# First head pair of an attention and two-MoE kernel: a new order of the start, head by head

## The chip, the cores and the metric

One core of a Trainium2 chip runs the whole program in one launch. The metric is device time in microseconds (us). The kernel before takes 651.89 us as the median of three runs (651.56 to 652.99). Its engines are TensorE (PE), VectorE (DVE), ScalarE (ACT), GpSimd (POOL) and SyncE (SP), which issues most transfers. PEld rows are TensorE's weight loads.

## The reference, cut to what matters

Three stages follow each other: cluster attention, a dense MLP, a routed MoE. The change touches the attention alone, and there its first pair of heads.

```python
q, k, v: (2, 8, 768, 64)   centroids: (8, 16, 64)
q_assign = argmax(q_n @ c_n.T); k_assign = argmax(k_n @ c_n.T)      # 16 clusters
mask = q_assign[:, :, :, None] == k_assign[:, :, None, :]
scores = where(mask, (q @ k.T) / 8, -1e9)
attn = exp(scores - max); attn /= sum + 1e-9
x = (attn @ v)  ->  (1536, 512)
h = x @ w_in; g = max(0.01 * h, h); x2 = g @ w_out                  # dense MLP
out = x2 + gate * (relu(x2 @ w1[e]) @ w2[e])   where x2 @ w_skip > 0, e = argmax(x2 @ w_gate)
```

## The kernel before, in words

**Tiling.** The 16 heads are worked off as 8 pairs p of two heads h. A pair takes 12 steps: a step s is 128 query rows of one head against all 768 keys. In pair 0 the steps alternate between the heads (h = 0, 1, 0, 1, ...). A step issues scores on PE (`sps`, four matmuls: two over the U tile with K = 80, two over the V tile with K = 128), a row maximum on DVE (`st`), an exponential on ACT (`pr`), and three steps later six transposes on PE (`tps`) whose copies ACT writes to `pt`. After six steps probabilities times v follow (`avps`). The `sps` tile has two buffers, so the scores of step s wait for the exponential of step s - 2.

**High and low parts.** q and k are fp32. Each is split into a high part in fp32r (a copy) and a low part (a subtraction). The tiles of pair p hold them by partitions: UA is head 0's high part (partitions 0 to 63), UB head 1's, VA and VB hold what the second pair of score matmuls multiplies. Rows 64 to 79 of UA and UB are the cluster masks: one-hot rows of the keys (0 or 1) and of the queries (0 or -2^60). A mask mismatch so lowers a score by 2^60.

**Preparation of a pair.** Load q and k (`nat`, for pair 0 `first` and a copy to `nat`); transpose on PE (`rawps`); copy on ACT (`raw`); split; exchange halves between the tiles by transfers on SP; multiply by the normalised centroids (`cblk`, result `asps`); copy on ACT (`sc`); transpose (`scps`); argmax in five DVE operations (maximum, equal, times `cw`, maximum, equal, result `oh`); masks. For pairs 1 to 7 the preparation is spread over the steps of the pair before by the tables PREP and PREP1. For pair 0 it stands ahead of the loop, lines 481 to 531, and PE's first scores come behind all of it: the order in the source is the order on each engine, since nothing reorders instructions.

**Ahead of the loop, in order.** SP issues `first` for q, the centroids (`cnat`), `first` for k, then pair 1's `natq` and `natk`. DVE normalises the centroids (`cst`, `cexp`). The high parts of q are made on POOL (line 199), those of k on ACT (line 197), all low parts on DVE (line 497), nine transfers of 192 KB exchange halves. `prep_cblk` (line 162) transposes `cexp` and copies it to `cblk`. One argmax serves both heads (lines 249 to 270). `mask_first` (line 273) makes the masks of head 0, then of head 1: 12 small transposes each (`mps`), a copy on ACT for the keys, one or two operations on DVE for the queries. Pair 1's q and k are transposed and copied there too.

## Time and profile before

| | before |
|---|---|
| median of 3 runs | 651.89 us |
| profiled execution, its own time | 651.22 us |
| its span, first to last instruction | 649.3 us |
| PE busy | 631.6 us, 97% of the span |
| DVE, ACT, POOL busy | 441.4, 420.8, 165.9 us |

The profiled execution's own time is 1.9 us longer than its span, and 0.7 us under the median of the runs. A time in a row is counted from the span's start. In the page's row of 40 slices PE has a 5 in the first one (16 us) and a 9 in all but the last after it: the start is the only stretch of some length in which PE is not busy. A busy PE is not PE at its peak, since matmuls are pipelined.

### The profile page before, as it was taken

The numbers are of one execution on the slowest core, as the hardware profiler recorded it, in microseconds if no ns is written. First come the engines' busy times: TensorE is split into PE (matmuls) and PEld (weight loads), VectorE is DVE, ScalarE is ACT, GpSimd is POOL, SyncE is SP. The second block draws the span as 40 slices with busy tenths as digits, with TensorE's granted clock in tenths as the row PEclk, the third lists the DMA queues.
The fourth block names the chain that finished last, engine by engine and source line by source line (L and its number), as shares of the span: only waits on it lengthen the run. The fifth ranks groups of instructions, "written<-read, shape, count | busy, mean of one in ns | idle before, by whom it ended". The sixth has DMA issues, their size and how long they took to land.

```text
span 649.3 us, 10059 instructions
## 1 busy us (share of the span) xinstructions
PE 631.6 (97%) x3599; PEld 489.9 (75%) x3599; DVE 441.4 (68%) x767; ACT 420.8 (65%) x829; POOL 165.9 (26%) x215
## 2 busy tenths in 40 slices
PE   5999999999999999999999999999999999999994
PEld 3777776776777676888888888888788878688874
DVE  6756868687777754988755355645566448999971
ACT  5788898898888885654544444444564346688860
POOL 4233647373655424300000000000000025004311
PEclk9999999999999999999999999999999999999998
DMA  8766566677656427223004000006234438999930
GB/s 194 183 188 160 144 167 186 154 202 187 189 174 172 156 71 276 97 98 100 1 1 194 1 1 0 2 12 248 108 131 150 140 131 304 365 349 373 360 136 28
DMA packets 63636, 99.53 MB, mean 153 GB/s; under 512 B 27697, under 2 KB 31763, under 8 KB 63200
## 3 DMA queue, kind: packets, MB, share of 16 engines
q1 hardware_dynamic: 60304, 90.62, 44.7%
q0 software_dynamic: 3280, 8.24, 3.7%
q8 instruction: 29, 0.48, 0.3%
q14 instruction: 23, 0.19, 0.1%
HBM read 72.73 MB, written 12.70 MB: 132 GB/s over the span
## 4 chain that ended last, share of the span: by engine, by line
PE 92%; ACT 2%; POOL 2%; DVE 1%; DMA 1%; issue 1%; SPq 0%; POOLq 0%
PE ups L669 20%; PE acc L775 19%; PE sps L371 10%; PE avps L443 10%; PE tps L428 8%; PE hps L1273 7%; PE yps L1304 7%; PE rawps L179 1%; PE hT L1285 1%; PE acc L1165 1%; PE x2T L859 1%; ACT pr L389 1%; PE asps L232 1%; DMA recip_scratch<-rrow 1%; PE scps L244 1%; PE xT L1034 1%
## 5 line engine op out<-in xcount | busy, mean ns | idle before, releaser
L374 DVE TENSOR_REDUCE st<-sps 128x1 f32<-128x768 f32 x96 | 91.6, 955 | 51.8 <-PE sps L371 50.9
L435 ACT ACTIVATE pt<-tps 128x384 f32<-128x384 f32 x192 | 85.5, 511 | 17.8 <-PE tps L428 16.6
L389 ACT ACTIVATE pr<-sps,st 128x768 f32<-128x768 f32 x96 | 88.2, 919 | 11.5 <-DVE st L374 11.2
L428 PE MATMUL tps<-ident,pr 128*128 128x128 f32 x576 | 79.0, 273 | 0.5 <-ACT pt L435 0.5
L669 PE MATMUL ups<-xh,whii 128*128 128x512 f32 x192 | 74.8, 390 | 0.0
L669 PE MATMUL ups<-xh,wloi 128*128 128x512 f32 x192 | 74.7, 389 | 0.0
L669 PE MATMUL ups<-xl,whii 128*128 128x512 f32 x192 | 74.7, 389 | 0.0
L775 PE MATMUL acc<-whio,gh 128*128 128x512 f32 x183 | 73.0, 399 | 0.0
L428 PEld LDWEIGHTS tps<-ident,pr 128*128 128x128 f32 x576 | 67.8, 140 | 5.8 <-ACT pt L435 1.6
L443 PE MATMUL avps<-pt,vnat 128*64 128x384 f32 x384 | 72.1, 498 | 0.0
L775 PE MATMUL acc<-whio,gl 128*128 128x512 f32 x183 | 71.4, 390 | 0.0
L775 PE MATMUL acc<-wloo,gh 128*128 128x512 f32 x183 | 71.3, 390 | 0.0
L760 ACT ACTIVATE gh<-g 128x512 fp32r<-128x512 f32 x48 | 30.4, 633 | 43.5 <-DVE g L759 43.5
L758 ACT ACTIVATE lk<-ups 128x512 f32<-128x512 f32 x48 | 28.4, 592 | 36.8 <-PE ups L669 30.3
L759 DVE TENSOR_TENSOR g<-ups,lk 128x512 f32<-128x512 f32 x48 | 33.0, 688 | 28.3 <-ACT lk L758 28.2
L762 DVE TENSOR_TENSOR gl<-g,gh 128x512 fp32r<-128x512 f32 x48 | 33.2, 691 | 25.2 <-ACT gh L760 25.2
L1013 POOL DMA_INDIRECT xe<-x_scratch,eix x1 | 1.2, 1165 | 190.0 <-DVE eix L1012 190.0
L646 DVE TENSOR_TENSOR wloi<-rawb,whii 128x512 fp32r<-128x512 f32 x36 | 24.8, 689 | 27.5 <-ACT whii L645 27.4
L443 PEld LDWEIGHTS avps<-pt,vnat 128*64 128x64 f32 x384 | 23.4, 136 | 25.5 <-issue 25.0
L669 PEld LDWEIGHTS ups<-xh,whii 128*128 128x128 f32 x192 | 36.0, 188 | 8.1 <-issue 0.6
L669 PEld LDWEIGHTS ups<-xl,whii 128*128 128x128 f32 x192 | 36.0, 188 | 7.5
L669 PEld LDWEIGHTS ups<-xh,wloi 128*128 128x128 f32 x192 | 36.0, 188 | 7.5
(303 smaller groups left out, 1358.3 us busy)
## 6 DMA issues: line engine op xcount, KB each, us to landing
rawb<-in_moe_w_dram SPq DMA_DIRECT2D x25, 1024.0 KB
rawa<-in_moe_w_dram SPq DMA_DIRECT2D x10, 1024.0 KB
stg<-in_moe_w_in_dram SPq DMA_DIRECT2D x16, 512.0 KB
stg<-in_moe_w_out_dram SPq DMA_DIRECT2D x16, 512.0 KB
UB<-UA SPq DMA_DIRECT2D x16, 192.0 KB
...
```

The costliest lines, as they stand in the source:

```text
L371: nc.tensor.matmul(ps[:, kh, 0:HS], lhsT=t[0:n, 0, qs], rhs=t[0:n, 1, kh * HS:(kh + 1) * HS], start=first, stop=not first)
L374: nc.vector.tensor_reduce(out=st[:, 0:1], in_=ps[:, :, 0:HS], axis=AX.XY, op=ALU.max, negate=True)
L389: nc.scalar.activation(out=pr, in_=ps[:, :, 0:HS], func=AF.Exp, bias=st[:, 0:1], accum_out=sm_t[g][:, 3 * h + j:3 * h + j + 1])
L428: nc.tensor.transpose(ps[:, t, :], pr[:, kh, t * P:(t + 1) * P], ident)
L435: nc.scalar.activation(out=pt[:, 3 * kh:3 * kh + 3, j, :], in_=t_t[s][kh], func=AF.Copy)
L443: nc.tensor.matmul(av_t[g][64 * h:64 * h + 64, :], lhsT=vnat[p][:, h, kt, :], rhs=pt_t[p, half, h][:, kt].rearrange("p j c -> p (j c)"), s ...
L669: nc.tensor.matmul(ps, lhsT=w[:, cc, :], rhs=x[:, blk, cc, :], start=(n == 0), stop=(n == 3 * KD - 1))
L759: nc.vector.tensor_tensor(out=g, in0=ps, in1=t, op=ALU.max)
L762: nc.vector.tensor_tensor(out=gl, in0=g, in1=_f(gh), op=ALU.subtract)
L775: nc.tensor.matmul(ps, lhsT=a[:, ts_], rhs=w, start=(fc == 0 and n == 0), stop=(fc == NFC - 1 and n == 2))
L1273: nc.tensor.matmul(ps, lhsT=x[:, c, :], rhs=w, start=(n == 0), stop=(n == len(mm) - 1))
L1304: nc.tensor.matmul(ps[:, cs], lhsT=x[:, f, :], rhs=w[:, cs], start=(h == 0 and f == 0 and n == 0), stop=(h == 1 and f == 3 and n == 2))
```

## The change

It changes the work ahead of the loop and steps 0 to 11.

- The centroids are loaded from ACT's queue instead of SP's, so k's load is the second on SP.
- The copies of head 0's q to `nat` move from DVE to POOL.
- Head by head: the first six steps are head 0's three, then head 1's three (`where`). Splits are made by head, over 64 partitions and 768 elements, instead of by half, over 128 partitions and 384 elements. Low parts of head 0 are on DVE, those of head 1 on POOL. Six transfers replace nine.
- The argmax is made by head with operations half as large: head 0's five ahead of step 0, head 1's first two ahead of step 0 and three behind the maxima of steps 0 and 1. Masks likewise; head 1's are made after step 2's scores. The copy of a key mask is shared between ACT and DVE.
- Pair 1's third and fourth group of transposes move from ahead of the loop into steps 1 and 2, as do the load of v (step 0) and of pair 2's q and k (step 2); pair 1's assignment moves from step 1 to step 3.
- Matmuls of the identity with itself (`wps`) are put on PE: 6 at the very start, 1, 2, 6 and 4 ahead of step 0, 5, 2 and 6 in steps 1 and 2. Their results are not used.
- The new tiles `first_lo` and `first_hi` take buffers of `pr`, as `lo_k` did.

DVE in the stretch of the splits and of the argmax, before. `VA` and `lo_k` are low parts, `cblk` the normalised centroids that PE waits for.

```order
L159 TENSOR_SCALAR cexp<-cnat,cst,par 128x64 x2
L497 TENSOR_TENSOR VA<-raw,UA 128x384
L165 COPY cblk<-cps 128x128
L497 TENSOR_TENSOR VA<-raw,UA 128x384
L497 TENSOR_TENSOR lo_k<-raw,UA 128x384 x2
L251 TENSOR_REDUCE mx<-scps 128x24
```

The same stretch of DVE after, to the end of head 0's masks.

```order
L159 TENSOR_SCALAR cexp<-cnat,cst,par 128x64 x2
L221 TENSOR_TENSOR VA<-raw,UA 64x768
L165 COPY cblk<-cps 128x128
L221 TENSOR_TENSOR first_lo<-raw,UA 64x768
L306 TENSOR_REDUCE mx_207<-scps 128x12
L311 TENSOR_TENSOR eq<-scps,mx_207 128x12x16
L315 TENSOR_TENSOR eq<-eq,cw 128x12x16
L317 TENSOR_REDUCE mx_207<-eq 128x12
L319 TENSOR_TENSOR oh<-eq,mx_207 128x12x16
L306 TENSOR_REDUCE mx_234<-scps 128x12
L336 CAST UA<-mps 16x384
L340 TENSOR_SCALAR UA<-mps 16x128
```

Two subtractions of 768 elements stand where four of 384 stood, and one of them is still ahead of `cblk`; the argmax has the same five operations at half the size.

DVE in steps 0 to 2 after, behind the masks that step 0 needs. `st` is a step's maximum, `UB` holds head 1's masks. Before, the two operations for UB's queries and UA's were ahead of step 0, and four maxima stood in a row.

```order
L311 TENSOR_TENSOR eq<-scps,mx_234 128x12x16
L431 TENSOR_REDUCE st<-sps 128x1 x2
L340 TENSOR_SCALAR UA<-mps 16x384
L315 TENSOR_TENSOR eq<-eq,cw 128x12x16
L317 TENSOR_REDUCE mx_234<-eq 128x12
L319 TENSOR_TENSOR oh<-eq,mx_234 128x12x16
L431 TENSOR_REDUCE st<-sps 128x1
L336 CAST UB<-mps 16x384
L340 TENSOR_SCALAR UB<-mps 16x768
L431 TENSOR_REDUCE st<-sps 128x1 x3
```

The three last operations of head 1's argmax and its masks now stand between the maxima of steps 1, 2 and 3.

ACT from step 0 on, after: `pr` is an exponential, `raw` a copy for pair 1, `UB` the first half of head 1's key mask, `pt` a copy of transposes, `sc` pair 1's assignment.

```order
L446 ACTIVATE pr,sm<-sps,st 128x768 x2
L196 ACTIVATE raw<-rawps 128x384
L335 ACTIVATE UB<-mps 16x384
L446 ACTIVATE pr,sm<-sps,st 128x768
L196 ACTIVATE raw<-rawps 128x384
L492 ACTIVATE pt_364<-tps 128x3x128 x2
L446 ACTIVATE pr,sm<-sps,st 128x768
L260 ACTIVATE sc<-asps 128x384
```

Before, `raw` and the masks came ahead of the first `pr`, and `sc` behind the second. The diff, without the parts that the list above tells in full:

```diff
@@ -190,13 +195,30 @@
         sc = SCALE if qk == 0 else 1.0
         nc.scalar.activation(out=raw_t[p][:, i, :], in_=ps, func=AF.Copy, scale=sc)
 
-    def first_hi(i):
-        qk, half = divmod(i, 2)
-        hi, src = uv_t[0][0][:, qk, half * HS:(half + 1) * HS], raw_t[0][:, i, :]
-        if qk:
-            nc.scalar.activation(out=hi, in_=src, func=AF.Copy)
-        else:
-            nc.gpsimd.tensor_scalar(out=hi, in0=src, scalar1=1.0, scalar2=1.0, op0=ALU.mult, op1=ALU.mult)
+    first_t = {}
+
+    def first_raw(qk, h):
+        return raw_t[0][64 * h:64 * h + 64, 2 * qk:2 * qk + 2, :].rearrange("p a b -> p (a b)")
+
+    def first_hi(qk, h, again=False):
+        U, W, X, Y = uv_t[0]
+        if qk == 0:
+            dst = (Y if h else U)[64 * h:64 * h + 64, 0, :]
+            nc.gpsimd.tensor_scalar(out=dst, in0=first_raw(0, h), scalar1=1.0, scalar2=1.0, op0=ALU.mult, op1=ALU.mult)
+        else:
+            dst = first_t["hi"][64:128] if h else (X if again else U)[0:64, 1, :]
+            nc.scalar.activation(out=dst, in_=first_raw(1, h), func=AF.Copy)
+
+    def first_lo(qk, h):
+        U, W, X, Y = uv_t[0]
+        if qk == 0:
+            hi = (Y if h else U)[64 * h:64 * h + 64, 0, :]
+            dst = first_t["lo"][64:128] if h else X[0:64, 0, :]
+        else:
+            hi = first_t["hi"][64:128] if h else U[0:64, 1, :]
+            dst = Y[64:128, 1, :] if h else first_t["lo"][0:64]
+        eng = nc.gpsimd if h else nc.vector
+        eng.tensor_tensor(out=dst, in0=first_raw(qk, h), in1=_f(hi), op=ALU.subtract)
 
     def raw_split(p, i):
         raw = raw_t[p]
@@ -270,21 +292,53 @@
                                 op=ALU.is_equal)
         oh_t[p] = oh
 
-    def mask_first(h):
-        U = uv_t[0][h]
+    def by_head(ap, h):
+        return ap.rearrange("p j (a h) c -> p j a h c", h=2)[:, :, :, h, :]
+
+    am0 = {}
+
+    def argmax_first(h, i):
+        V = nc.vector
+        sc = by_head(ps_prep["am"], h)
+        sh = [P, 3, 4, NC_]
+        if i == 0:
+            am0["m", h] = att_a.tile([P, 3, 4], F32, tag="mx0", name="mx0", bufs=2)
+            V.tensor_reduce(out=am0["m", h], in_=sc, axis=AX.X, op=ALU.max)
+        elif i == 1:
+            if "e" not in am0:
+                am0["e"] = att_a.tile([P, 3, 8, NC_], F32, tag="eq", name="eq")
+                oh_t[0] = att_a.tile([P, 3, 8, NC_], BF16, tag="oh", name="oh")
+            V.tensor_tensor(out=by_head(am0["e"], h), in0=sc, in1=am0["m", h].unsqueeze(3).to_broadcast(sh),
+                            op=ALU.is_equal)
+        elif i == 2:
+            eq = by_head(am0["e"], h)
+            V.tensor_tensor(out=eq, in0=eq, in1=cw[:, 0:4].unsqueeze(1).to_broadcast(sh), op=ALU.mult)
+        elif i == 3:
+            V.tensor_reduce(out=am0["m", h], in_=by_head(am0["e"], h), axis=AX.X, op=ALU.max)
+        else:
+            V.tensor_tensor(out=by_head(oh_t[0], h), in0=by_head(am0["e"], h),
+                            in1=am0["m", h].unsqueeze(3).to_broadcast(sh), op=ALU.is_equal)
+
+    mf_t = {}
+
+    def mask_first_pe(h):
         for qk in (1, 0):
-            ps = (ps_m if h else ps_t)([P, S], "mps", BF16) if qk or not h else ps_a([P, S], "mps", BF16)
+            ps = ps_t([P, S], "mps", BF16)
             for i in range(2):
                 for j in range(3):
                     o = (3 * i + j) * P
                     nc.tensor.transpose(ps[64:64 + NC_, o:o + P], oh_t[0][:, j, 4 * qk + 2 * i + h, :], identb)
-            ps = ps[64:64 + NC_, :]
-            if qk:
-                nc.scalar.activation(out=U[64:64 + NC_, 1, :], in_=ps, func=AF.Copy)
-            else:
-                for cs in (slice(0, HS), slice(HS, S)) if h == 0 else (slice(0, S),):
-                    nc.vector.tensor_scalar(out=U[64:64 + NC_, 0, cs], in0=ps[:, cs], scalar1=BIG, scalar2=-BIG,
-                                            op0=ALU.mult, op1=ALU.add)
+            mf_t[h, qk] = ps[64:64 + NC_, :]
+
+    def mask_first_k(h):
+        U, ps = uv_t[0][h], mf_t[h, 1]
+        nc.scalar.activation(out=U[64:64 + NC_, 1, 0:HS], in_=ps[:, 0:HS], func=AF.Copy)
+        nc.vector.tensor_copy(U[64:64 + NC_, 1, HS:S], ps[:, HS:S])
+
+    def mask_first_q(h, a, z):
+        U, ps = uv_t[0][h], mf_t[h, 0]
+        nc.vector.tensor_scalar(out=U[64:64 + NC_, 0, a:z], in0=ps[:, a:z], scalar1=BIG, scalar2=-BIG,
+                                op0=ALU.mult, op1=ALU.add)
 
     def mask_pe(p):
         ps = (ps_t if p == 2 else ps_m)([P, 3, P], "ohps", BF16)
@@ -325,8 +379,9 @@
     PREP = plan(1)
     PREP0 = [(3, "a0", assign_act, None), (3, "pb", argmax_pe, None), (4, "d", argmax_0, None), (4, "d", argmax_1, None),
              (5, "d", argmax_2, None), (6, "d", argmax_3, None)]
-    PREP1 = [(1, "pb", assign_pe, None), (2, "a0", assign_act, None), (2, "pb", argmax_pe, None), (3, "pb", argmax_0, None), (4, "pb", argmax_1, None), (5, "d", argmax_2, None), (6, "pb", argmax_3, None), (7, "pb", mask_pe, None), (8, "d", mask_dve, None),
-             (8, "d", mask_dma, None)]
+    PREP1 = [(3, "pb", assign_pe, None), (4, "a0", assign_act, None), (4, "pb", argmax_pe, None),
+             (5, "d", argmax_0, None), (5, "d", argmax_1, None), (6, "d", argmax_2, None), (7, "d", argmax_3, None),
+             (8, "pb", mask_pe, None), (8, "pb", mask_dve, None), (8, "pb", mask_dma, None)]
     PREPS = {0: PREP0, 1: PREP1, 2: plan(5)}
 
     def prep(p, r, slot):
@@ -359,6 +414,8 @@
         p, r = divmod(s, 12)
         half, r = divmod(r, 6)
         j, h = divmod(r, 2)
+        if s < 6:
+            h, j = divmod(s, 3)
         return p, half, j, h
 
     def st_scores(s):
...
@@ -485,50 +547,47 @@
     for i in range(4):
         raw_pe(0, i)
         raw_act(0, i)
-    for i in range(4):
-        first_hi(i)
-    UA, UB, VA, VB = uv_t[0]
-
-    lo_k = att.tile([P, 2, HS], F32R, tag="pr", name="lo_k", bufs=4)
-
-    def first_lo(qk, halves=(0, 1)):
-        for half in halves:
-            cs = slice(half * HS, (half + 1) * HS)
-            nc.vector.tensor_tensor(out=lo_k[:, half, :] if qk else VA[:, 0, cs], in0=raw_t[0][:, 2 * qk + half, :],
-                                    in1=_f(UA[:, qk, cs]), op=ALU.subtract)
-
-    Uq, Wq, Xq, Yq = (_f(t[:, 0, :]) for t in (UA, UB, VA, VB))
-    Uk, Wk, Xk, Yk = (_f(t[:, 1, :]) for t in (UA, UB, VA, VB))
-    nc.sync.dma_start(Wq[0:64], Uq[64:128])
-    nc.sync.dma_start(Yq[64:128], Uq[64:128])
-    nc.sync.dma_start(Wk[0:64], Uk[64:128])
-    nc.sync.dma_start(Yk[0:64], Uk[64:128])
-    first_lo(0, (0,))
+    U, W, X, Y = uv_t[0]
+    for nm in ("lo", "hi"):
+        t = att.tile([P, 2, HS], F32R, tag="pr", name="first_" + nm, bufs=4)
+        first_t[nm] = t.rearrange("p a b -> p (a b)")
+    first_hi(0, 0)
+    nc.sync.dma_start(_f(X[64:128, 0, :]), _f(U[0:64, 0, :]))
+    first_hi(0, 1)
+    nc.sync.dma_start(_f(W[0:64, 0, :]), _f(Y[64:128, 0, :]))
+    first_lo(0, 0)
     prep_cblk()
-    first_lo(0, (1,))
-    nc.sync.dma_start(Yq[0:64], Xq[64:128])
-    nc.gpsimd.dma_start(Xk[0:64], Uk[0:64])
+    warm_pe(1, wps)
+    first_hi(1, 0)
+    first_hi(1, 1)
     assign_pe(0)
-    first_lo(1)
-    lo_kf = _f(lo_k.rearrange("p a b -> p (a b)"))
-    nc.sync.dma_start(Xk[64:128], lo_kf[0:64])
-    nc.sync.dma_start(Yk[64:128], lo_kf[64:128])
-    nc.sync.dma_start(Xq[64:128], Uq[0:64])
+    warm_pe(2, wps)
+    first_lo(1, 0)
+    nc.sync.dma_start(_f(X[64:128, 1, :]), _f(first_t["lo"][0:64]))
     prep(0, 3, "a0")
+    first_hi(1, 0, True)
+    nc.sync.dma_start(_f(W[0:64, 1, :]), _f(first_t["hi"][64:128]))
+    nc.sync.dma_start(_f(Y[0:64, 1, :]), _f(first_t["hi"][64:128]))
+    first_lo(0, 1)
+    nc.sync.dma_start(_f(Y[0:64, 0, :]), _f(first_t["lo"][64:128]))
     nc.scalar.activation(out=warm, in_=warm, func=AF.Exp)
     prep(0, 3, "pb")
-    for r in range(4, 7):
-        for slot in ("d", "pb"):
-            prep(0, r, slot)
-    load_v(0)
-    for i in range(4):
-        raw_pe(1, i)
-        raw_act(1, i)
-    load_qk(2)
-    mask_first(0)
-    mask_first(1)
-    for i in range(4):
-        split_first(1, i)
+    for i in range(5):
+        argmax_first(0, i)
+    raw_pe(1, 0)
+    raw_pe(1, 1)
+    wps = ps_a([P, P], "wps")
+    warm_pe(6, wps)
+    argmax_first(1, 0)
+    first_lo(1, 1)
+    mask_first_pe(0)
+    mask_first_k(0)
+    mask_first_q(0, 0, P)
+    mask_first_q(0, P, HS)
+    raw_act(1, 0)
+    raw_act(1, 1)
+    argmax_first(1, 1)
+    warm_pe(4, wps)
 
     chunks = {}
     ring_b = [None]
@@ -690,6 +749,29 @@
         p, r = divmod(s, 12)
         if s < NSTEP:
             st_scores(s)
+        if s == 0:
+            load_v(0)
+        elif s == 1:
+            raw_pe(1, 2)
+            warm_pe(5, wps)
+            mask_first_q(0, HS, S)
+            for i in range(2, 5):
+                argmax_first(1, i)
+        elif s == 2:
+            raw_act(1, 2)
+            raw_pe(1, 3)
+            warm_pe(2, wps)
+            mask_first_pe(1)
+            warm_pe(6, wps)
+            mask_first_k(1)
+            mask_first_q(1, 0, S)
+            load_qk(2)
+            for i in range(2):
+                split_first(1, i)
+        elif s == 3:
+            raw_act(1, 3)
+            for i in range(2, 4):
+                split_first(1, i)
         conv_step(s, 0)
         preps(p, r, "a0")
         preps(p, r, "pa")

```

## Rows read from the trace of the kernel before

**Rows 1.** Waits of PE from 24 to 645 us: total, times, longest us
```profile
PE tps L428 <- ACT pt L435: 0.5, 2, 0.3
PE rcps L406 <- ACT raw L191: 0.3, 1, 0.3
```

**Rows 2.** Windows: length, busy us (instructions) by engine, granted clock, DMA share, GB/s
```profile
12.00:16.00 4.00, 2.86 (x17) 2.46 (x16) 3.39 (x5) 2.39 (x6) 2.63 (x4) 1.00 1.03 236
24.00:28.00 4.00, 3.99 (x29) 3.44 (x27) 3.30 (x5) 4.00 (x11) 0.59 (x1) 1.00 0.56 139
```

**Rows 3.** Timeline of PE: start us, us, engine, line, operation, count, [idle before]
```profile
8.85 1.51 PE L232 MATMUL asps<-raw,cblk 128*32 128x384 f32 x8 [0.58 <-DVE cblk L165]
10.98 0.90 PE L244 MATMUL scps<-ident,sc 128*128 128x128 f32 x3 [0.63 <-ACT sc L238]
12.96 1.49 PE L179 MATMUL rawps<-ident,natk 128*128 128x128 f32 x6
15.58 2.73 PE L280 MATMUL mps<-identb,oh 128*16 128x128 bf16 x24 [1.14 <-DVE oh L269]
18.24 1.01 PE L371 MATMUL sps<-UA 80*128 80x384 f32 x2
...
23.41 0.60 PE L371 MATMUL sps<-UB 80*128 80x384 f32 x2
...
24.19 0.81 PE L428 MATMUL tps<-ident,pr 128*128 128x128 f32 x6
24.89 0.62 PE L371 MATMUL sps<-UA 80*128 80x384 f32 x2
...
33.10 0.62 PE L371 MATMUL sps<-UB 80*128 80x384 f32 x2
```

**Rows 4.** Timeline of SP: issues of the first loads
```profile
1.31 0.46 SPq L107 DMA_DIRECT2D cnat<-in_centroids_dram  x1
1.80 0.43 SPq L103 DMA_DIRECT2D first<-in_k_dram  x1
```

**Rows 5.** Timeline of ACT, start to step 1
```profile
6.04 0.61 ACT L475 ACTIVATE nat<-first 128x192 f32<-128x192 f32 x2 [1.15 <-DMA first<-in_k_dram]
...
6.56 2.03 ACT L191 ACTIVATE raw<-rawps 128x384 f32<-128x384 f32 x4
...
10.44 0.49 ACT L238 ACTIVATE sc<-asps 128x384 f32<-128x384 f32 x1 [1.03 <-PE asps L232]
...
20.80 0.90 ACT L389 ACTIVATE pr<-sps,st 128x768 f32<-128x768 f32 x1 [2.29 <-DVE st L374]
...
21.69 0.89 ACT L389 ACTIVATE pr<-sps,st 128x768 f32<-128x768 f32 x1
```

**Rows 6.** Timeline of DVE and POOL, splits and argmax of pair 0
```profile
7.11 0.99 POOL L199 TENSOR_SCALAR UA<-raw 128x384 fp32r<-128x384 f32 x2 [0.33 <-ACT raw L191]
...
7.65 0.85 DVE L497 TENSOR_TENSOR VA<-raw,UA 128x384 fp32r<-128x384 f32 x1 [0.53 <-POOL UA L199]
...
8.42 0.28 DVE L165 COPY cblk<-cps 128x128 f32<-128x128 f32 x1
...
8.62 0.54 DVE L497 TENSOR_TENSOR VA<-raw,UA 128x384 fp32r<-128x384 f32 x1
...
11.92 0.56 DVE L251 TENSOR_REDUCE mx<-scps 128x24 f32<-128x384 f32 x1 [1.82 <-PE scps L244]
...
13.11 0.56 DVE L259 TENSOR_TENSOR eq<-eq,cw 128x384 f32<-128x384 f32 x1
...
14.12 1.00 POOL L209 TENSOR_TENSOR VA<-raw,UA 128x384 fp32r<-128x384 f32 x1
14.28 1.24 DVE L269 TENSOR_TENSOR oh<-eq,mx 128x384 bf16<-128x384 f32 x1
```

**Rows 7.** Timeline of DVE, masks of pair 0 and the first two maxima
```profile
17.07 1.03 DVE L286 TENSOR_SCALAR UA<-mps 16x384 fp32r<-16x384 bf16 x2 [1.54 <-PE mps L280]
18.35 0.95 DVE L286 TENSOR_SCALAR UB<-mps 16x768 fp32r<-16x768 bf16 x1 [0.25 <-PE mps L280]
19.80 1.82 DVE L374 TENSOR_REDUCE st<-sps 128x1 f32<-128x768 f32 x2 [0.50 <-PE sps L371]
```

More of the change, by code (lines that the diff above doesn't have):

```diff
@@ L106, in load_qk @@
             if p == 0 and nm == "q":
-                nc.sync.dma_start(cnat, centroids.rearrange("h c d -> (h c) d"))
+                nc.scalar.dma_start(cnat, centroids.rearrange("h c d -> (h c) d"))
     def load_v(p):
@@ L176, in raw_pe @@
         src = nat["qk"[qk], p]
-        ps = ((ps_t, ps_t, ps_m, ps_a)[i] if p == 0 else ((ps_t, ps_t, ps_a, ps_t)[i] if p == 1 else ps_m))([P, 3, P], "rawps")
+        if p == 1 and i < 2:
+            if i == 0:
+                ps_prep["raw2"] = ps_s("rawps")
+            ps = ps_prep["raw2"][:, i, 0:HS].rearrange("p (j c) -> p j c", c=P)
+        else:
+            ps = ((ps_t, ps_t, ps_m, ps_a)[i] if p == 0 else ps_m)([P, 3, P], "rawps")
         for j in range(3):
@@ L271, in argmax_3 @@
         oh_t[p] = oh
-    def mask_first(h):
-        U = uv_t[0][h]
+    def by_head(ap, h):
[5 more added lines that the diff above has]
+        sh = [P, 3, 4, NC_]
+        if i == 0:
+            am0["m", h] = att_a.tile([P, 3, 4], F32, tag="mx0", name="mx0", bufs=2)
[16 more added lines that the diff above has]
+    def mask_first_pe(h):
         for qk in (1, 0):
-            ps = (ps_m if h else ps_t)([P, S], "mps", BF16) if qk or not h else ps_a([P, S], "mps", BF16)
+            ps = ps_t([P, S], "mps", BF16)
             for i in range(2):
@@ L475, in first_copy, with warm_pe @@
                 nc.scalar.activation(out=dst, in_=src, func=AF.Copy)
-            elif nm == "q":
-                nc.vector.tensor_copy(dst, src)
             else:
                 nc.gpsimd.tensor_scalar(out=dst, in0=src, scalar1=1.0, scalar2=1.0, op0=ALU.mult, op1=ALU.mult)
+    wps = ps_s("wps")[:, 0, 0:P]
+    def warm_pe(n, ps):
+        for _ in range(n):
+            nc.tensor.matmul(ps, lhsT=ident, rhs=ident, start=True, stop=True)
+    warm_pe(6, wps)
     first_copy(0)
@@ L692 @@
             st_scores(s)
+        if s == 0:
[11 more added lines that the diff above has]
+            mask_first_pe(1)
+            warm_pe(6, wps)
+            mask_first_k(1)
[7 more added lines that the diff above has]
+                split_first(1, i)
         conv_step(s, 0)
```

## The prediction, made before the changed kernel was run

> **What bounds the kernel now.** I read the page's 40 slices first, then the waits of PE, the windows, and the timelines of the start. The slices show one PE gap of some length, the first 16 us. Behind 24 us PE waits for others three times and 0.8 us in all [rows 1], so a shift of the point at which PE's steady work begins is a shift of the end: nothing later has slack to take it up. Which point is that? Step 0's scores begin at 18.24, step 3's at 23.41, step 9's at 33.10 [rows 3]. From 24 to 28 us both PE (3.99 of 4) and ACT (4.00 of 4) are full [rows 2]; a step there takes (33.10 - 23.41) / 6 = 1.62 us. So step 0 alone decides nothing. What counts is when step 3, whose transposes open ACT's full stretch, can run, and how ACT and PE go from there to step 9. I work out these three points.
>
> The granted clock reads 1.00 (the 2.4 GHz level) from the start [rows 2], yet six transposes take 1.49 us at 12.96 and 0.81 at 24.19 [rows 3]. I take early PE durations as they stand and later ones for the case that the added matmuls bring the fast level sooner.
>
> **Step 0's start.** *Load of k.* The centroids' issue leaves SP, so k is issued 0.49 earlier (1.31 instead of 1.80) [rows 4]. k lands by 6.04 [rows 5]; the gain is between 0 and 0.49, I take 0.34: 5.7, since DMA engines were already loaded.
>
> *To the splits.* ACT: two copies as before, 6.56 - 6.04 = 0.52, then two raw copies of 2.03 / 4 = 0.51 [rows 5]: 7.25. The old split began after one of them, the new one needs both halves. POOL's high part of q, head 0: 768 elements a partition. A 384 one takes 0.50 [rows 6], so between 0.50 and 1.0; I take 0.85: 8.1, and head 1's 8.95.
>
> *DVE and POOL meet.* At 7.65 a DVE subtraction of 384 took 0.85 beside POOL, 0.54 alone at 8.62; POOL's second copy ran until 8.10, 0.45 into it. At 14.28 the last argmax operation took 1.24, a sister operation at 13.11 0.56; POOL's subtraction ran from 14.12 to 15.12 [rows 6]. Both ends lie 0.40 behind the end of POOL's instruction. So I let a DVE operation with two SBUF inputs wait for the end of POOL's, and POOL's new ones are long: a 384 subtraction takes 1.00, so 768 takes 1.0 to 2.0, and I take 1.85.
>
> The Trainium skill (SBUF — State Buffer, section "SBUF: two separate sides") says that the port pair which the two share is locked for a whole instruction and that the loser fully blocks. By that rule the waits below are in full; were they only of the observed size, 0.3 to 0.7 each, the sum would be that of the second rival.
>
> Head 0's low part on DVE asks at 8.1, waits for head 1's high part until 8.95, takes 0.8 more (half of it is 0.40): 9.8. Only then comes `cblk`, 0.28: 10.1, against 8.70 before. PE's `asps` runs 1.51 [rows 3] or, at the fast level, 1.51 x 0.81 / 1.49 = 0.82: 10.95 to 11.6. `sc` 0.49 [rows 5], `scps` 0.90 [rows 3] or 0.5: 12.0 to 13.0, against 11.88. Meanwhile POOL's low part of q, head 1, runs from 9.8 to 11.65, DVE's low part of k waits for it and ends at 12.5. Then POOL's second low part runs 12.5 to 14.35.
>
> *Argmax.* Five operations of half size. A full one takes 0.56 [rows 6], so 0.28 to 0.56; I take 0.36 with 0.02 between. Two run from 12.6 to 13.35; the third multiplies two SBUF tiles and waits for POOL until 14.35; three end at 15.45. Before, `oh` ended at 15.52. Halving gains 1.0 us of work and the two waits take it back.
>
> *Masks.* Before, 24 transposes took 2.73 [rows 3]. Six of the keys take a quarter, 0.68, or 0.37 at the fast level; I take 0.55: 16.05. ACT copies half of the key mask, 0.49: 16.55; DVE's half stands behind a wait for ACT in the new order, and a 384 one takes 1.03 / 2 = 0.52 [rows 7]: 17.1. The first 128 queries, a third of that and a fixed part, 0.3: **17.4**. Step 0 begins 0.8 earlier. The four identity matmuls cost at least a transpose each, 0.81 / 6 = 0.14, and at most two, 0.27, as a full fp32 matmul shows two records (`asps` x8 for four). I take 0.25: 1.0 in all, done by 17.5, hidden, if the fast level holds. Step 0's last operand is the transfer of k's low part, issued at 12.5 with 4.9 us to go; hidden.
>
> **From step 0 to step 3.** Before: 23.41 - 18.24 = 5.17. After, counted from step 0: the first maximum began 19.80 - 18.24 = 1.56 behind the scores, at the fast level I take 1.0; two take 1.82 [rows 7]: 2.8. ACT's exponential 0 begins at 2.0; two of 0.89 [rows 5] end at 3.8. Only then comes the copy of pair 1's third group, 0.49: 4.3. PE's fourth group waits for it (three transposes, 0.4): 4.7. Two identity matmuls, 0.5, stand between: 5.2. Six key masks of head 1, 0.5: 5.7. ACT's half copy 0.49: 6.2. DVE's half 0.52: 6.75. Queries of head 1, 768 wide, 0.95 [rows 7]: 7.7. Step 3 multiplies UB and waits for that: **7.7**, step 3 at 25.1. Head 1's argmax (done by 4.5) and the six identity matmuls (5.7 + 0.4 + 1.5 = 7.6) are just hidden. So head 1's masks, which stood ahead of step 0 on an idle machine, now lie on the way to step 3: 2.5 us lost, 0.8 gained, 1.7 late.
>
> **From step 3 to step 9.** Before 9.69. Step 4's scores began 24.89 - 23.41 = 1.48 behind step 3's. Now `asps` of pair 1 stands between them, 0.85 of PE while ACT has just begun its first `pt`: 2.3, and ACT's `sc`, 0.49, comes into the full stretch. Bounds: 0.49 if PE's part is hidden, 0.85 + 0.49 = 1.3 if neither is. I take 0.8.
>
> **Sum.** -0.8 + 2.5 + 0.8 = 2.5 us. 651.22 + 2.5 = 653.7 for a profiled execution; the median of the runs stands 0.67 higher, so **654.4**.
>
> *Costed at nothing.* The 6 identity matmuls at the start (PE idle until its first transposes, behind q's load; without that cover 1.6 to 3.0 us). The copies of q on POOL (POOL is idle until k lands; raw copies wait for k in any case). Six transfers for nine: before, VA's matmuls followed UA's without a wait, so no transfer ended last. The later loads: v and pair 2's q are first used behind step 9's scores, at 33.10 or later; if SP's queue held them past that, PE would stand. The 16-wide masks of pair 1 come a step later (step 8), and step 12 needs them some 7 us on.
>
> **Rivals.**
> *The early start is kept* (other side). If the distance from step 0 to step 3 stayed at 5.2, because head 1's argmax and masks fit between maxima and exponentials, and step 3 to 9 at 9.7, the change would be worth what step 0 gains. With POOL's waits small (`oh` at 13.4), step 0 comes at 15.4, 2.8 earlier: 651.9 - 2.8 = 649.1. For it: ACT and PE have gaps between 20 and 24 us. Against: the chain above runs over one engine after the other. It decides from a distance under 7.0.
> *POOL's waits are small.* Step 0 at 15.7, but the distance 7.7 and the 0.8 stay: -2.5 + 2.5 + 0.8 = +0.8, 652.7. For it: the waits seen were 0.3 and 0.7, not 1.5. Against: they fit an end set by POOL's instruction.
> *PE stays at the slow level past step 0.* Before, transposes were slow until 14.5 though PE was busy 2.86 of 4 us [rows 2], and the first scores were too (1.01 against 0.62) [rows 3]. Then the 12 masks take 1.4, the four identity matmuls 2.0 and those of steps 1 and 2 twice theirs, no longer hidden: about 1.0 at step 0, 1.0 more to step 3: 656.4. For it: matmuls come in short pieces with waits between. Against: 13 added ones fall in the pauses ahead of step 0, beside the 6 at the start.
> *The transfers come late*, the last (low part of head 1's q, issued near 11.7) behind the others: no time up to step 3, since that is at 25; it does nothing.
>
> **How the numbers follow.** Two tenths of a per cent, 1.3 us, is what a measurement of this kernel can tell from no change. Forecast 0.50, 654.4, of itself 653.2 to 655.8 (k's landing 0.3 either way, 0.4 to 1.3 behind step 3, POOL's size 0.5). Small waits 0.20, 652.7, on the edge of no change. Early start kept 0.17, 649.1 with a foot to 651. Slow level 0.13, 656.4. Faster by over 0.2%: the early start, 0.17. Within: most of small waits and a little of the forecast, 0.25. Slower: 0.58. The range leaves out the better half of the early start and the worst of the slow level: 650.3 to 656.6.
>
> **What would show it.** In the profile of the changed kernel: `cblk` at 10.1 and not at 8.4; subtractions on DVE of 1.6 to 2.5 us beside POOL's; `oh` of head 0 near 15.4; step 0 at 17.4; the last mask operation of UB's queries just ahead of step 3; step 3 near 25; step 9 near 35.6, and from there the same distances as before. I am wrong if step 3 comes ahead of 23.4, or if PE waits behind 36 us.

## The result, and the profile of the changed kernel

The changed kernel takes 655.81 us (median of 7 runs, 654.18 to 656.96); the kernel before takes 651.89 us beside it. The ratio is 1.0051, 95% interval 1.0035 to 1.0067: slower by 3.3 us by the ratio and by 3.9 by the two medians. That is the forecast's side (2.5 us), and 1.4 us above its 654.4. The profiled execution took 654.18 us, span 652.5 (651.22 and 649.3 before), so 3.0 more than the profiled one of before.

PE's timeline in the changed kernel, start to step 9:

```profile
4.95 1.85 PE L184 MATMUL rawps<-ident,nat 128*128 128x128 f32 x12 [0.59 <-POOL nat L534]
...
9.84 0.85 PE L254 MATMUL asps<-raw,cblk 128*32 128x384 f32 x8 [1.23 <-DVE cblk L165]
...
11.32 0.55 PE L266 MATMUL scps<-ident,sc 128*128 128x128 f32 x3
...
14.70 0.84 PE L330 MATMUL mps<-identb,oh 128*16 128x128 bf16 x12 [0.84 <-DVE oh L319]
15.47 1.16 PE L540 MATMUL wps<-ident 128*128 128x128 f32 x8
16.66 0.58 PE L428 MATMUL sps<-UA 80*128 80x384 f32 x2
...
21.86 0.84 PE L330 MATMUL mps<-identb,oh 128*16 128x128 bf16 x12
22.62 1.60 PE L540 MATMUL wps<-ident 128*128 128x128 f32 x12
24.44 0.58 PE L428 MATMUL sps<-UB 80*128 80x384 f32 x2 [0.21 <-ACT raw L196]
...
25.21 0.82 PE L485 MATMUL tps<-ident,pr 128*128 128x128 f32 x6
25.96 0.85 PE L254 MATMUL asps<-raw,cblk 128*32 128x384 f32 x8
26.74 0.62 PE L428 MATMUL sps<-UB 80*128 80x384 f32 x2
...
35.14 0.62 PE L428 MATMUL sps<-UB 80*128 80x384 f32 x2
```

Beside [rows 3]: step 0 at 16.66 and not 18.24, step 3 at 24.44 and not 23.41, step 9 at 35.14 and not 33.10. So 1.58 us are gained ahead of step 0, 2.61 lost between steps 0 and 3 (7.78 for 5.17), 1.01 between steps 3 and 9 (10.70 for 9.69). The twelve transposes of 4.95 take 1.85, six took 1.51 before; `asps` takes 0.85 for 1.51: PE is at the 2.4 GHz level early. The trace's clock records agree: the first one, a rise to full clock, stands at 5.5 us here and at 19.5 us before. Ahead of it the clock column prints 1.00 with no record behind it.

DVE and POOL of the changed kernel, splits and argmax (beside [rows 6]):

```profile
7.81 0.88 POOL L207 TENSOR_SCALAR VB<-raw 64x768 fp32r<-64x768 f32 x1
7.92 1.57 DVE L221 TENSOR_TENSOR VA<-raw,UA 64x768 fp32r<-64x768 f32 x1
8.78 2.39 POOL L221 TENSOR_TENSOR first_lo<-raw,VB 64x768 fp32r<-64x768 f32 x1
9.42 0.27 DVE L165 COPY cblk<-cps 128x128 f32<-128x128 f32 x1
9.62 2.36 DVE L221 TENSOR_TENSOR first_lo<-raw,UA 64x768 fp32r<-64x768 f32 x1
11.13 2.52 POOL L221 TENSOR_TENSOR VB<-raw,first_hi 64x768 fp32r<-64x768 f32 x1
...
12.69 1.18 DVE L315 TENSOR_TENSOR eq<-eq,cw 128x192 f32<-128x192 f32 x1
...
14.29 0.36 DVE L319 TENSOR_TENSOR oh<-eq,mx 128x192 bf16<-128x192 f32 x1
```

Read the ends, in order: POOL 8.69, DVE 9.49, POOL 11.17, DVE 11.98, POOL 13.65, DVE 13.87. Each ends a fixed time behind the end of the other engine's: DVE's subtractions 0.80, POOL's 1.68, the half-size product 0.22. They take turns, whole instruction by whole instruction; a row's length contains the wait. `cblk`'s copy, which reads PSUM, took its usual 0.27 us in the middle of POOL's 2.39.

ACT, PE and DVE from step 0 to step 3 of the changed kernel:

```profile
18.62 0.90 ACT L446 ACTIVATE pr<-sps,st 128x768 f32<-128x768 f32 x1 [2.00 <-DVE st L431]
...
19.52 0.90 ACT L446 ACTIVATE pr<-sps,st 128x768 f32<-128x768 f32 x1
...
20.39 0.49 ACT L196 ACTIVATE raw<-rawps 128x384 f32<-128x384 f32 x1
...
20.85 0.36 DVE L319 TENSOR_TENSOR oh<-eq,mx 128x192 bf16<-128x192 f32 x1
...
20.93 0.55 PE L184 MATMUL rawps<-ident,natk 128*128 128x128 f32 x3 [0.30 <-ACT raw L196]
...
21.32 0.61 PE L540 MATMUL wps<-ident 128*128 128x128 f32 x4
...
22.40 0.48 ACT L335 ACTIVATE UB<-mps 16x384 fp32r<-16x384 bf16 x1 [1.52 <-PE mps L330]
...
22.91 0.56 DVE L336 CAST UB<-mps 16x384 fp32r<-16x384 bf16 x1 [0.71 <-ACT UB L335]
...
23.39 0.95 DVE L340 TENSOR_SCALAR UB<-mps 16x768 fp32r<-16x768 bf16 x1
...
23.80 0.48 ACT L196 ACTIVATE raw<-rawps 128x384 f32<-128x384 f32 x1
```

This is the chain that was forecast: exponentials 0 and 1, the copy at 20.39, PE's fourth group of transposes at 20.93, two identity matmuls at 21.32, the transposes of head 1's masks at 21.86, ACT's half copy to 22.88. Then DVE's half to 23.47 and head 1's query masks to 24.34; step 3 follows at 24.44. (Its row names ACT's copy, which ended at 24.28; the masks that step 3 reads ended last.)

### The profile page after: what moved, and what is told of

Same layout as the page of the kernel before. It is cut to its first block, busy times and chain, and to the rows that moved or that the text cites. A ratio compares the mean times of both kernels' runs of the same rounds, so it can differ in the third digit from the quotient of the medians.

```text
span 652.5 us, 10186 instructions
## 1 busy us (share of the span) xinstructions
PE 636.3 (98%) x3663; PEld 494.8 (76%) x3663; DVE 443.7 (68%) x771; ACT 421.9 (65%) x830; POOL 169.5 (26%) x218
## 4 chain that ended last, share of the span: by engine, by line
PE 85%; DVE 5%; ACT 3%; DMA 2%; POOL 2%; issue 1%; SPq 1%; POOLq 0%; DVEq 0%; ACTq 0%
PE ups L728 20%; PE acc L857 19%; PE avps L500 8%; PE sps L428 8%; PE hps L1355 7%; PE yps L1386 7%; PE tps L485 6%; ACT pr L446 1%; PE rawps L184 1%; PE hT L1367 1%; PE acc L1247 1%; DVE st L431 1%; PE x2T L941 1%; DMA stg<-in_moe_w_out_dram 1%; DMA stg<-in_moe_w_in_dram 1%
```

## The experiments

They ran in five batches, each on one chip beside the kernel before, which took 651.64 to 652.15 us there; a ratio is to the kernel before of the same batch. Step 0 and the distances are from one profiled execution of each kernel. In runs 2, 3, 7, 8 and 11 the granted clock falls to about half for part of steps 0 to 9 (0.50 from 20 to 26 us in run 3, for example), so their distances hold PE rows of up to twice the length.

| run | us | ratio to before (95%) | step 0 | 0 to 3 | 3 to 9 |
|---|---|---|---|---|---|
| before | 651.89 | | 18.24 | 5.17 | 9.69 |
| changed | 655.81 | 1.0051 (1.0035, 1.0067) | 16.66 | 7.78 | 10.70 |
| 1 changed, no identity matmuls | 658.34 | 1.0091 (1.0068, 1.0114) | 17.02 | 9.08 | 12.60 |
| 2 changed, none in steps 1, 2 | 656.07 | 1.0067 (1.0054, 1.0080) | 17.10 | 7.33 | 12.26 |
| 3 before + identity matmuls | 658.50 | 1.0097 (1.0080, 1.0115) | 17.07 | 8.46 | 10.12 |
| 4 as 3, PSUM places kept | 653.39 | 1.0027 (1.0016, 1.0037) | 17.94 | 6.33 | 9.69 |
| 5 changed, PSUM places kept | 653.89 | 1.0037 (1.0024, 1.0049) | 16.68 | 7.77 | 10.71 |
| 6 before + late assignment | 653.30 | 1.0028 (1.0017, 1.0039) | 18.54 | 4.20 | 11.17 |
| 7 changed, masks ahead of step 0 | 658.81 | 1.0104 (1.0086, 1.0122) | 22.13 | 5.82 | 10.71 |
| 8 as 4 + order of heads, transfers | 652.85 | 1.0017 (1.0005, 1.0030) | 19.70 | 5.00 | 10.13 |
| 9 as 8, transfers mended, gate | 654.22 | 1.0037 (1.0024, 1.0049) | 18.05 | 6.25 | 9.71 |
| 10 as 9, no identity matmuls | 651.36 | 0.9994 (0.9985, 1.0002) | 17.90 | 5.18 | 9.70 |
| 11 changed, losses taken back | 654.72 | 1.0037 (1.0024, 1.0051) | 16.38 | 9.55 | 9.99 |
| 12 as 11, `raw` of pair 1 moved | 650.55 | 0.9981 (0.9972, 0.9991) | 15.63 | 5.38 | 9.69 |

**Run 1.** In the changed kernel:

```
-        for _ in range(n):
+        for _ in range(0):
```

> The changed kernel without any of its identity matmuls (26 fewer on PE). Theory (they bring the fast level, which is worth 1.5 us ahead of step 0 and hides what they cost): asps 1.5 and not 0.85, step 0 at 18.0 to 18.8 (16.66 with them), distance 0 to 3 of 7.8 to 8.5, time 657 to 658.5, slower than the changed kernel by 1.5 to 2.5 us. Rival (they cost PE time in steps 1 and 2 and gain nothing): step 0 at 16.5, distance 7.0, time near 655, 0.5 to 1 us under the changed kernel.

Slower than the changed kernel by 2.5 us, as the theory had it (the two intervals lie apart), but not where it said: step 0 only moved to 17.02. `asps` did take 1.51, yet here DVE's first subtraction came 0.05 us ahead of POOL's second copy and POOL waited, so `cblk` was there 0.7 earlier. The cost lies behind step 0: transposes at 1.49 per six until 29 us, distances 9.08 and 12.60. The trace's first clock record, the rise to full clock, stands at 30.2 us.

**Run 2.** `warm_pe(5, wps)`, `warm_pe(2, wps)` and `warm_pe(6, wps)` of steps 1 and 2 taken out.

> The changed kernel without the 13 identity matmuls of steps 1 and 2; those at the start and ahead of step 0 stay. Theory (PE must be kept busy through steps 1 and 2 too, since it falls to the slow level in the waits there): step 0 at 16.5 to 16.8, distance 0 to 3 of 8.2 to 9.0, tps behind step 3 in 1.5 per six; time 656.5 to 658.5. Rival (they stand on the chain to step 3 and the level holds without them): distance 7.0 to 7.4, time 654.9 to 655.4.

PE in run 2, around step 3, and DVE's one-hot ahead of it:

```profile
21.29 0.36 DVE L319 TENSOR_TENSOR oh<-eq,mx 128x192 bf16<-128x192 f32 x1
...
21.37 0.55 PE L184 MATMUL rawps<-ident,natk 128*128 128x128 f32 x3 [0.28 <-ACT raw L196]
...
21.85 0.84 PE L330 MATMUL mps<-identb,oh 128*16 128x128 bf16 x12
...
24.43 0.58 PE L428 MATMUL sps<-UB 80*128 80x384 f32 x2 [1.74 <-ACT raw L196]
24.85 0.58 PE L428 MATMUL sps<-VB 128*128 128x384 f32 x2
25.23 1.48 PE L485 MATMUL tps<-ident,pr 128*128 128x128 f32 x6
26.65 1.51 PE L254 MATMUL asps<-raw,cblk 128*32 128x384 f32 x8
28.09 0.83 PE L428 MATMUL sps<-UB 80*128 80x384 f32 x2
```

Step 3 comes at the same time as with them (24.43 and 24.44), but step 0 came 0.44 us later here, at 17.10, though the two programs are the same up to step 1: k's copies began at 5.80 and not at 5.45, and DVE came ahead of POOL as in run 1. From step 0 on, the distance is 0.45 shorter, 7.33 for 7.78. From head 0's masks up to the copy of the third group every row lies 0.44 behind that of the changed kernel; then the mask transposes start at 21.85 behind DVE's one-hot (done at 21.65), where with the two identity matmuls ahead of them they started at 21.86 although the one-hot was done at 21.21. So the two stand on the chain, as the prediction had it, and cost 0.45 of its length. What the rest buys is seen behind step 3: after a pause of 1.74 us the granted clock is 0.50 (26 to 28 us), six transposes take 1.48 and `asps` 1.51, and step 9 is 1.55 us later. Each theory had half of it: the rival the chain, the theory the level. The time lies between their two ranges, and is not told apart from the changed kernel's (the intervals overlap).

**Runs 3 and 4.** In the kernel before, 6 identity matmuls at the start, 1, 2, 6 and 4 further on. Run 4 differs in the tiles they write:

```
-    wps = ps_s("wps")[:, 0, 0:P]
+    wps = ps_t([P, 3, P], "wps")[:, 0, :]      # the first six; ps_s from the second place on
```

> The kernel before with the identity matmuls alone: 6 at the start, 1 and 2 around the first assignment matmuls, 6 ahead of the 24 mask transposes, 4 behind them. Theory (the added matmuls bring PE's fast level ahead of step 0, and that is the part of the change that gains): asps of pair 0 takes 0.85 and not 1.51, scps 0.55 and not 0.90, the 24 mask transposes 1.5 to 2 and not 2.73; step 0 near 16.8 (18.24 before), the distances 0 to 3 and 3 to 9 stay near 5.1 and 9.7; time 650.2 to 650.9, below the kernel before by 1.0 to 1.7 us. Rival (they are only more work for PE, and what set step 0 in the kernel before was DVE and ACT): step 0 at 18.0 to 18.8, time 651.7 to 652.5.

> The kernel before with the same identity matmuls, but the first six write a bank of tag T, so that the PSUM tags get the addresses they have in the kernel before (T, M, A, S and not S first); from the second place on a tile of tag S is taken. Theory (4.8 us of the 7.9 that the identity matmuls cost came from the place of S: the third ups tile then lies on the bank of the second, PE waits 3.06 us for its g at 264 us and falls to the slow level): that wait is gone, no granted clock under 1.00 near 265 us, time 653.0 to 654.3 (658.5). What stays, some 2.5 us, comes from steps 0 to 3, where VA's last transfer lands 2.3 us late. Rival (the wait comes from the shift of the attention by 3 us, as the weights' stream then stands otherwise): the wait stays, 657.5 to 659.

Run 3 gained the 1.17 us at step 0 and lost 6.9 us in all (658.50 against 651.64): neither theory. Two waits did it, each with PE at a lower clock behind it (granted clock 0.50 from 20 to 26 us behind the first). PE in run 3, at step 0 and at the seam to the MLP (`ups` and `acc` are the PSUM tiles of the MLP's two products):

```profile
17.07 0.59 PE L371 MATMUL sps<-UA 80*128 80x384 f32 x2
19.97 0.98 PE L371 MATMUL sps<-VA 128*128 128x384 f32 x2 [2.31 <-DMA VA<-UA]
...
260.83 0.39 PE L680 MATMUL ups<-xh,wloi 128*128 128x512 f32 x1
264.28 0.50 PE L680 MATMUL ups<-xh,whii 128*128 128x512 f32 x1 [3.06 <-DVE g L770]
```

The windows of run 3 there (columns: stretch, length, busy time of PE, PEld, DVE, ACT, POOL, granted clock, DMA):

```profile
260.00:264.00 4.00, 1.22 (x6) 0.68 (x4) 3.38 (x4) 2.11 (x4) 2.78 (x3) 1.00 0.02 8
264.00:268.00 4.00, 3.72 (x11) 2.97 (x12) 2.22 (x4) 2.25 (x4) 3.68 (x19) 0.67 0.00 0
268.00:272.00 4.00, 4.00 (x17) 3.24 (x17) 2.40 (x5) 1.57 (x3) 0.00 (x0) 0.90 0.00 0
```

The second wait is one of place. PSUM tiles are placed by tag, in the order in which tags are first used. Before, that is T, M, A, S. A first tile of tag S puts S on banks 0 to 3. The first two `ups` tiles are S tiles, and the MLP's own tiles start again at bank 0: in run 3 the third `ups` tile lies (by the addresses in the built program) on the bank of the second and waits until DVE has read it; then PE works at a granted clock of 0.67 and 0.90. With the places of before the wait and the lower clock are gone, and run 4 takes 5.1 us less than run 3, inside its forecast. What is left at the start is the first wait: a transfer of 192 KB, issued at 15.9, now ends last (1.50 us in run 4). Step 0 of run 4 comes at 17.94, 0.87 later than in run 3 with the same matmuls: the granted clock, up at 5.4 us, reads 0.60 from 8 to 12 us there, and `asps` took 1.51.

**Run 5.** The same edit in the changed kernel.

> The changed kernel with its first six identity matmuls on a bank of tag T, so that the PSUM tags lie as in the kernel before. Theory (0.3 to 0.5 us of the change's loss come from the place of S, where the first acc tile lies on the bank of the second ups tile): the wait of acc for g (0.46) at 263.5 us is gone, time 654.9 to 655.6. Rival (that shift is a matter of DVE and POOL only): the wait stays, 655.6 to 656.2.

In the changed kernel the first `acc` tile lay on that bank; the 0.46 us between the starts of `ups` at 263.36 and `acc` at 263.82 are 0.22 here (263.56 and 263.78), the usual spacing. So the wait was 0.24 us and not 0.46; the span is 0.3 us shorter. The median is 1.9 us lower (0.9 by the ratios), more than either theory said, but the two intervals overlap.

**Run 6.** Pair 1's table alone, in the kernel before:

```
-    PREP1 = [(1, "pb", assign_pe, None), (2, "a0", assign_act, None), ...
+    PREP1 = [(3, "pb", assign_pe, None), (4, "a0", assign_act, None), ...
```

> The kernel before with pair 1's assignment, argmax and masks alone at their later steps, as the changed kernel has them. Theory (this work is hidden between steps 1 and 3, where ACT and PE have gaps, and in the full stretch behind step 3 it costs its size): steps 0 and 3 as before or up to 0.3 earlier, distance 3 to 9 of 10.4 to 10.8 (9.69 before), time 652.4 to 653.0, 0.5 to 1.1 us above the kernel before. Rival (the 1.0 us from step 3 to step 9 comes from the splits and loads of the new steps 1 to 3): distance 9.7, time as before.

Distance 3 to 9 grew by 1.48, more than forecast; step 3 came 0.67 earlier, since `asps` and `scps` no longer stood ahead of it. At step 9 that leaves 0.81 us; the time is 1.8 us higher (1.1 to 2.5), more than the 0.5 to 1.1 forecast.

**Run 7.** In the changed kernel, head 1's argmax and masks ahead of step 0:

```
-    argmax_first(1, 1)
+    for i in range(1, 5):
+        argmax_first(1, i)
+    mask_first_q(0, HS, S)
+    mask_first_pe(1)
+    mask_first_k(1)
+    mask_first_q(1, 0, S)
     warm_pe(4, wps)
```

> The changed kernel with head 1's last argmax operations, its mask transposes and its mask copies, and the second half of head 0's query mask, moved ahead of step 0; the six identity matmuls that stood behind head 1's masks go. Theory (these stand on the chain from step 0 to step 3, and what step 0 gained is what this part lost): step 0 near 19.5, distance 0 to 3 of 5.0 to 5.8 (7.78), step 3 at 24.4 to 25.2, time within 0.8 us of the changed kernel: the same work in another place. Rival (the work has free engine time ahead of step 0 and only the chain through steps 1 and 2 is dear): step 0 at 17.5 to 18, distance 5.3, step 3 at 23, time 1.0 to 1.8 us below the changed kernel.

Both theories fell. The distance shrank to 5.82, but step 0 came at 22.13: PE waited 3.42 us for head 1's `oh`, because in this order it stands on DVE behind head 0's masks and again behind POOL's instructions. Behind that wait the granted clock is 0.50 (22 to 24 us). Put back that way, the work costs 5.5 us where it had cost 2.6.

**Runs 8, 9 and 10.** The way from the other side, kernel before plus parts: `where` by heads, and the transfer that empties VA's lower half (`VB<-VA`) issued first. Run 9 moves the key transfers up again, adds seven matmuls, three of them in one more pause, and holds POOL's splits of pair 1 until `oh` is done:

```
+    gate = att_a.tile([P, 3, 8], F32, tag="gate", name="gate")
+    nc.gpsimd.tensor_copy(gate, oh_t[0][:, :, :, 0])
     for i in range(4):
         split_first(1, i)
```

> The kernel before with identity matmuls and PSUM places as in the run above, and two more parts of the change: steps 0 to 5 take head 0's three query blocks first, and VA's two q transfers are issued ahead of those that only head 1 reads. Both heads' argmax and masks stay ahead of step 0, and pair 1's assignment at step 1. Theory (the gain is the clock and the early transfer for head 0; the loss of the change is head 1's chain and the late assignment): step 0 at 16.8 to 17.2, no wait for a transfer, distance 0 to 3 of 4.6 to 5.2, distance 3 to 9 of 9.5 to 9.9, time 649.6 to 650.6. Rival (the distance 0 to 3 grows when step 0 comes early, since the raw copies of pair 1 and the transfers then meet it): distance 6.0 or more, time 651 to 652.5.

> The version that the runs so far point to. The kernel before, PSUM places kept, with: identity matmuls in more of PE's pauses (6 at the start, 3 while k lands, 3 and 2 around the first assignment, 8 ahead of the masks, 4 behind); VA's transfer out of its own lower half issued first of all, the key transfers behind it but ahead of the first waiting one (the last run had them too late, and the key masks waited for them until 18.8); head 0's three blocks first in steps 0 to 5; and GpSimd's splits of pair 1 held until head 0's and 1's one-hot is done, so that they don't lock DVE out of its last argmax operation. Theory (step 0 is set by one chain of small waits, each now shortened: asps 0.85 for 1.51, last argmax operation 0.56 for 1.24, VA's transfer landed by 17.5): step 0 at 16.4 to 17.3, distance 0 to 3 of 4.6 to 5.4, 3 to 9 of 9.6 to 9.9; time 650.0 to 651.0, 0.8 to 1.8 us under the kernel before. Rival (each shortened wait uncovers the next, the transfers first of all, and step 3 stays at 23.4 or later): 651.5 to 652.8.

> The same without any identity matmul. Theory (the matmuls are worth 1.0 to 1.5 us in it): asps 1.51, scps 0.90, 24 mask transposes 2.7, step 0 at 17.4 to 17.9, distance 0 to 3 near 5.2, 651.2 to 652.0. Rival (the level of PE ahead of step 0 doesn't decide, since DVE, ACT and the transfers do): within 0.4 us of the run beside it.

Runs 8 and 9 missed every range given for their time; run 9's rival had the mechanism (each shortened wait uncovers the next, step 3 at 24.30). In run 8 the key masks' copy waited 4.75 us for a transfer that reads the rows they overwrite (my reorder had put it late). In run 9 the argmax was as short as hoped (last operation 0.56 at 13.61), but that copy still waited for transfers until 17.15, and VA's transfer, issued at 14.36, held PE until 20.06. Run 10 landed in its theory's ranges (step 0 at 17.90, 651.36 us), but by luck: the theory made the matmuls worth 1.0 to 1.5 us, and without them the kernel is 2.9 us faster than run 9 and no faster than before. `scps` (0.55) and the 24 mask transposes (1.51) were fast without any, where it had 0.90 and 2.7. So in this kernel the matmuls were worth less than nothing. There VA's transfer, issued at 14.50, held PE only until 18.86; why the same transfer took 5.7 us in run 9 and 4.4 here stays open. In none of the seven kernels with nine transfers does step 1 come ahead of 19.28.

**Runs 11 and 12.** The changed kernel, six transfers kept, with: PSUM places as before; `cblk` ahead of the first subtraction; both heads' argmax in a row; POOL's two low parts of head 1 behind it, by the same gate; each key mask in one copy on ACT; head 1's masks and pair 1's raw copies in the gaps of step 0; PREP1 as before; no matmuls in steps 1 and 2. Run 12 moves one tile:

```
-            raw_t[p] = att_a.tile([P, 4, HS], F32, tag="raw", name="raw")
+            if p == 1:
+                t = att.tile([P, NT, 3, P], F32, tag="pt0", name="raw1", bufs=2).rearrange("p a b c -> p (a b c)")
+                raw_t[p] = t[:, 0:4 * HS].rearrange("p (a b) -> p a b", b=HS)
+            else:
+                raw_t[p] = att_a.tile([P, 4, HS], F32, tag="raw", name="raw")
```

This buffer of tag `pt0` is free until step 9.

> The changed kernel with each of its losses taken back where it was found, and its six transfers kept (they are what lets step 0 come early: with the nine of before VA's last transfer landed at 18.9 to 20.1). PSUM tags placed as before; cblk ahead of DVE's first subtraction; GpSimd's two low parts of head 1 held until both heads' one-hot is done, so that they lock DVE out of nothing; both heads' argmax in one row on DVE; the key masks on ACT in one piece each; head 1's masks and pair 1's raw copies between the masks of head 0 and step 0's exponential; pair 1's assignment at step 1 again; no identity matmuls in steps 1 and 2. Theory (the losses were head 1's chain behind the exponentials, 2.6, the late assignment, 1.0, and the place of S, 0.3, and all can be had without giving up the early start): step 0 at 15.8 to 16.8, distance 0 to 3 of 4.7 to 5.5, distance 3 to 9 of 9.5 to 9.9, time 649.4 to 650.8. Rival (the early start is worth nothing by itself: PE falls to the slow level without the matmuls in steps 1 and 2, or the low part of head 1's q, now issued near 17, lands behind step 3's place): distance 0 to 3 of 6.5 or more, 651.5 to 654.

> The last run with one tile moved: pair 1's raw copies go into a free buffer of tag pt0 and not into pair 0's raw tile, whose last reader is GpSimd's low part of head 1 (held until 19.1 there, so that ACT stood 4.5 us and PE 2.7). Theory (that was the one wait that the held low parts made; all else of the forecast for the last run stands): step 0 at 16.2 to 16.6 as there, step 1 within 1.4 of it (4.6 there), distance 0 to 3 of 4.7 to 5.5, 3 to 9 of 9.6 to 9.9, time 649.6 to 650.8. Rival (PE's level: in the pauses of steps 1 and 2 without identity matmuls it falls, and step 3 comes no sooner than 22.8): 651.5 to 653.

ACT in run 11:

```profile
19.13 1.25 ACT L196 ACTIVATE raw<-rawps 128x384 f32<-128x384 f32 x3 [4.50 <-POOL VB L221]
20.41 0.80 ACT L335 ACTIVATE UB<-mps 16x768 fp32r<-16x768 bf16 x1
```

Step 0 came at 16.38 as hoped; then pair 1's copy waited for the tile whose last reader had been moved back, PE 2.70 us for that copy, and behind it the granted clock is 0.50 (20 to 26 us). So neither of its theories held. With another tile, PE in run 12:

```profile
15.63 0.60 PE L430 MATMUL sps<-UA 80*128 80x384 f32 x2
...
21.01 0.59 PE L430 MATMUL sps<-UB 80*128 80x384 f32 x2
...
30.70 0.62 PE L430 MATMUL sps<-UB 80*128 80x384 f32 x2
...
38.88 0.59 PE L430 MATMUL sps<-UA 80*128 80x384 f32 x2 [0.59 <-DMA UA<-mk]
```

Step 0 is 2.61 earlier than before, step 9 still 2.40. It came in its forecast for the two distances and for the time. It is the one version whose interval lies under the kernel before: 650.55 us, 0.19% less (0.09 to 0.28%), at the edge of the 0.2% that the prediction calls measurable, and, by the two ratios, some 0.7% under the changed one. A third of the 2.40 goes at step 12, where PE waits for pair 1's masks (issued at 33.99, behind step 8's work).

## Why the prediction was right, point by point

- *The clock.* The prediction read the column's 1.00 as the 2.4 GHz level from the start, and left the slow transposes unexplained. That 1.00 is no reading: the trace of the kernel before has no clock record ahead of 19.5 us. Its rows at either length, from which it worked, were the right guide.
- *Load of k.* Copies at 5.45 (5.7 said); over the seven kernels with this order of loads they began at 5.32 to 5.80. Not foreseen: q's copies began at 4.45 (4.30 to 4.56), where all runs built on the kernel before have 3.9.
- *DVE and POOL meet.* Right in full: the waits are those of a whole instruction. By the Trainium skill (SBUF — State Buffer, section "SBUF: two separate sides") the loser of the shared port pair blocks until the other lets go. The ends above agree, 0.80 us behind POOL's end for 768 elements. POOL's subtraction was sized at 1.85; alone it takes 1.82 (run 12), behind the end of DVE's 1.68, as DVE's takes 0.94 alone and 0.80 behind POOL's: the first 0.14 us of either fall into the wait. Which engine is first is a matter of 0.05 us (run 1), and decides whether `cblk` comes at 8.98 or 9.69.
- *Step 0.* 16.66 for 17.4. The gain came out 0.74 larger because two terms were taken too long: k's load, by which DVE's first subtraction ended 0.3 sooner, and POOL's two subtractions, 0.34 together. `scps` (0.55) is not on this path, since the third argmax operation waited for POOL until 13.65. The mechanisms held; the size of the gain is good to 0.4 us only, as run 2 shows with the same program at 17.10.
- *Step 0 to step 3.* 7.78 for 7.7, by the chain named, link by link: counted from step 0, PE's fourth group ends at 4.82 (4.7 said), the masks' transposes start at 5.20 (5.2), ACT's half copy ends at 6.22 (6.2), DVE's at 6.81 (6.75), the queries' masks at 7.68 (7.7). The two identity matmuls are one of the links: without them the distance is 7.33 (run 2).
- *Step 3 to step 9.* 10.70 for 10.5. Run 6 shows the late assignment alone to cost 1.48 there.
- *Costed at nothing: the transfers.* "No transfer ended last" was read from a step 0 at 18.24, with VA's matmuls at 19.04. It is not true of an earlier step 0: in runs 3, 4, 9 and 10, with nine transfers, PE waited 2.31, 1.50, 1.43 and 0.38 us for the last. The changed kernel, with six, has no such wait; that its early start stands on this is likely, but no run changes the number of transfers alone.
- *Costed at nothing: the six identity matmuls at the start.* They are hidden on PE, but their tile moved tag S, which cost 0.24 us at 263 us here and 3.06 in run 3.
- *"From there the same distances."* The step that failed. The shift is 2.04 at step 9, 2.90 at the last step of the attention (243.42 for 240.52), 3.2 behind the seam. The sum said 2.5: 0.46 too much up to step 9 and 1.1 missing behind it, so that the total came near by two errors of opposite sign, which is luck. Of the 1.4 us by which the median lies above the forecast, 1.0 is that the changed kernel's median stands 1.6 above its profiled execution, where 0.67 was taken. The seam is shown (run 5). The 0.9 us between come in jumps of 0.1 to 0.4, some of them back, some at steps where other kernels have them too (20, 86). They are not in PE's listed waits, which are 1.1 us behind 36 us against 0.8 behind 24 us before. All twelve experiments show the same sign from step 9 to step 95, from 0.3 us (run 10) to 2.1 us (run 12, where a gain of 2.40 shrinks to 0.30). They are all read against one profiled execution of the kernel before, which lies 0.7 us under its median, so that a part of that size may be its own. What goes beyond it says that a shift of the start isn't carried unchanged through the attention. Why was not settled, beyond the masks of run 12.
- *The rivals.* "The early start is kept" was the opportunity: not in this change, but run 12 has distances of 5.38 and 9.69 and still gains 1.2 us, not the 2.8 worked out, for the reason just told. "The slow level" is what run 1 is, and run 2 behind step 3. "POOL's waits are small" is excluded by the ends above.
